# One fixed list orders TensorE, ScalarE and VectorE through the first block of an attention and two-MLP kernel

## The chip, the cores and the metric

The kernel runs on one core of one Trainium2 chip. The metric is the device time of one execution in microseconds (us). The engines are TensorE (PE), VectorE (DVE), ScalarE (ACT), GpSimd (POOL) and SyncE (SP), which issues the transfers.

## The reference, cut to what matters

Three stages follow each other: attention inside chunks of 64 positions, an MLP with a SiLU, and an MLP with a softmax-weighted activation and a normalization. All of it has to come out with float32 accuracy.

```python
# q, k, v: (8, 8, 576, 64); chunks of 64 along the sequence
scores = scale * np.matmul(q_c, k_c.transpose(0, 1, 2, 4, 3))
scores = scores - np.max(scores, axis=-1, keepdims=True)
attn = np.exp(scores)
attn = attn / (np.sum(attn, axis=-1, keepdims=True) + 1e-09)
out = np.matmul(attn, v_c)
# x: (4608, 512); w_in (512, 2048), w_out (2048, 512)
h = x @ w_in
g = h * (1.0 / (1.0 + np.exp(-h)))
x = g @ w_out
# w_in (512, 1024), w_out (1024, 512), g_ln (1024)
h = x @ w_in
e = np.exp(h - np.max(h, axis=-1, keepdims=True))
solu = h * e / (np.sum(e, axis=-1, keepdims=True) + 1e-09)
mu = np.mean(solu, axis=-1, keepdims=True)
var = np.mean((solu - mu) ** 2, axis=-1, keepdims=True)
out = (solu - mu) / np.sqrt(var + 1e-06) * g_ln @ w_out
```

## The kernel before, in words

**Numbers.** Each float32 operand of a matmul is split in two float16 halves, a high one (ACT, L114) and a low one, the rest (POOL at L118 where no gain is applied, else DVE at L119). A product is three matmuls: high by high, high by low, low by high.

**Blocks.** The 4608 rows are taken in nine blocks of 512, each of four tiles of 128. A block b goes through attention, the first layer (16 groups `h_0` to `h_15` of 12 matmuls with w1 and a Silu: `h_group`, and then the halves of its result g: `g_split`), the second layer (w2: `x_part`, four results in two halves of 24 matmuls each), the third (w3: `m_h`, one call a tile, with row maxima, exponentials and the statistics of the normalization on DVE and ACT) and the fourth (w4: `m_out`). The attention of block b + 1 (scores, `a_norm`, P·V with `a_pv`) stands between the parts of block b's second layer; the third and fourth layer of block b - 1 stand between the groups of block b: `m_h` ahead of groups 5, 7, 9 and 11, `m_out` ahead of 13 and 15 and behind 15. Blocks 2 to 8 use another form of the first two layers, with sums of weights that are made during block 1.

**Weights.** The weights come once, as 48 pieces in a line: 0 to 15 are w1, 16 to 31 w2, 32 to 39 w3, 40 to 47 w4. A piece is loaded as 64-bit words and decoded to float32 in four steps: `d1` scales one half on ACT (L133), `d2` shifts and joins the bits with three operations of DVE (L140, L141, L143) and issues the load of a later piece on SP, `d3` makes the halves (ACT at L114, then POOL at L118, or DVE at L119 for w4, which has a gain). `weights(n)` does `d3 d1 d2` n times, each on the oldest piece that waits for it. So the decoding has to stay ahead of its reader: `h_f` needs piece f, the parts of the second layer pieces 16 to 31, `m_h` all of 32 to 39, `m_out` all of 40 to 47.

**What sets the order.** A scheduler puts the instructions of each engine in order by their place in the program and by priorities; `tc.high_priority(offset=-50)` puts what stands inside it later. Only for the start, up to block 0's first group, does a list fix the order: `START` names steps, and each step is issued behind the last instruction of the steps before it, engine by engine (`queue` and `tc.issue_after`). Behind it, `NW0`, `NX`, `NW1` and `NX1` say how many pieces are decoded beside each group of block 0, each step of its second layer, each group of block 1 and each step of that block's second layer. `START` leaves six pieces with d1, five with d2 and four with d3 done; block 0 ends with 37 of d1 and 35 of d3.

**Names in rows.** wst is a loaded piece, wp and wy its decoded forms, w, w2t, w3q, w4h and w4l the halves of weights; qk, qb, qbl and kb belong to the q and k of a tile, vbh and vbl to v, ae and pT to its scores; x is an input of the first layer, g its result; e, u, uT, nmu, c and dv belong to the third layer's activation; y, wq and ws to the sums of weights.

## Time and profile before

| what | value |
|---|---|
| time, median of 3 runs | 1172.4 us (1171.79 to 1173.0) |
| the profiled execution | 1173.64 us, span 1171.9 us |
| mean granted clock of TensorE in it | 0.993 |
| busy in the span: PE, DVE, ACT, POOL | 1123.9, 917.4, 803.3, 250.4 us |

The span is what the profiler's records cover; the execution's own time lies 1.7 us above it. A row of a timeline gives the start in us from the span's start, the duration in us, the engine, the line of the kernel, the operation, what it writes and reads, and shapes. The bracket at its end is the time for which the engine had been idle, and the instruction that ended this, as inferred from semaphores.

### The profile page before, as it was taken

The numbers are of one execution on the slowest core, as the hardware profiler recorded it, in microseconds if no ns is written. First come the engines' busy times: TensorE is split into PE (matmuls) and PEld (weight loads), VectorE is DVE, ScalarE is ACT, GpSimd is POOL, SyncE is SP. The second block draws the span as 40 slices with busy tenths as digits, with TensorE's granted clock in tenths as the row PEclk, the third lists the DMA queues.
The fourth block names the chain that finished last, engine by engine and source line by source line (L and its number), as shares of the span: only waits on it lengthen the run. The fifth ranks groups of instructions, "written<-read, shape, count | busy, mean of one in ns | idle before, by whom it ended". The sixth has DMA issues, their size and how long they took to land.

```text
span 1171.9 us, 23546 instructions
## 1 busy us (share of the span) xinstructions
PE 1123.9 (96%) x9036; PEld 767.0 (65%) x9036; DVE 917.4 (78%) x1639; ACT 803.3 (69%) x1460; POOL 250.4 (21%) x243
## 2 busy tenths in 40 slices
PE   7899898998999999999999999999999999999998
PEld 5344343444657865887678767876787777777853
DVE  6898998587678788889778987898689868886453
ACT  6986678675667777856775687568756875587253
POOL 3655323344101510021003100310021002100001
PEclk8999999999999999999999999999999999999999
DMA  7657488543537654786568557856776667565604
GB/s 280 217 186 209 150 234 270 166 140 113 140 113 222 180 157 132 200 228 179 150 189 235 175 157 192 230 169 160 179 235 173 162 177 223 168 163 145 207 19 117
DMA packets 205169, 209.18 MB, mean 178 GB/s; under 512 B 120192, under 2 KB 130432, under 8 KB 205056
## 3 DMA queue, kind: packets, MB, share of 16 engines
q1 hardware_dynamic: 205056, 207.68, 61.8%
q8 instruction: 70, 1.15, 0.4%
q14 instruction: 43, 0.35, 0.1%
HBM read 156.24 MB, written 24.12 MB: 154 GB/s over the span
## 4 chain that ended last, share of the span: by engine, by line
PE 64%; DVE 13%; ACT 9%; issue 6%; DMA 5%; POOL 2%; ACTq 0%; SPq 0%; POOLq 0%; DVEq 0%
PE o_ps L894 5%; PE o_ps L887 5%; PE o_ps L886 5%; PE pa L655 4%; PE pa L654 4%; PE pa L656 4%; PE pa L547 3%; PE pa L549 3%; PE pa L548 3%; PE pa L781 2%; PE pa L779 2%; PE pa L780 2%; DVE vbl L119 2%; PE pb L549 2%; PE pb L547 2%
## 5 line engine op out<-in xcount | busy, mean ns | idle before, releaser
L114 ACT ACTIVATE q<-hc 128x512 f16<-128x512 f32 x196 | 120.5, 627 | 42.8 <-DVE hc L634 15.6
L119 DVE SCALAR_TENSOR_TENSOR q<-hc,q 128x512 f16<-128x512 f32 x196 | 137.9, 719 | 10.9 <-ACT q L114 8.7
L118 POOL TENSOR_TENSOR qbl<-qk,qbh 64x512 f16<-64x512 f32 x54 | 71.2, 1319 | 264.7 <-ACT qbh L114 220.3
L654 PE MATMUL pa<-q,ring 128*128 128x256 f16 x448 | 122.1, 273 | 0.0
L656 PE MATMUL pa<-q,ring 128*128 128x256 f16 x448 | 122.1, 273 | 0.0
L655 PE MATMUL pa<-q,ring 128*128 128x256 f16 x448 | 122.1, 273 | 0.0
L886 PE MATMUL o_ps<-w4h,uT 128*128 128x512 f16 x288 | 109.1, 379 | 0.3 <-DVE e L837 0.3
L887 PE MATMUL o_ps<-w4l,uT 128*128 128x512 f16 x288 | 109.2, 379 | 0.0
L850 POOL TENSOR_TENSOR c<-c,mhalf 128x2 f32<-128x2 f32 (+1 forms) x22 | 14.1, 639 | 387.3 <-DVE c L849 385.1
L548 PEld LDWEIGHTS <-ring 128*128 128x128 f16 x784 | 77.0, 98 | 16.7 <-issue 6.1
L547 PEld LDWEIGHTS <-ring 128*128 128x128 f16 x784 | 77.0, 98 | 11.3 <-DMA ring<-w1s 0.7
L655 PEld LDWEIGHTS <-ring 128*128 128x128 f16 x784 | 76.7, 98 | 11.1
L654 PEld LDWEIGHTS <-ring 128*128 128x128 f16 x784 | 76.7, 98 | 11.1
L549 PEld LDWEIGHTS <-ring 128*128 128x128 f16 x784 | 77.0, 98 | 9.2
L656 PEld LDWEIGHTS <-ring 128*128 128x128 f16 x784 | 76.7, 98 | 8.8
L894 PE MATMUL o_ps<-w4h,uT 128*128 128x512 f16 x288 | 70.2, 379 | 0.0
L547 PE MATMUL pa<-xb,ring 128*128 128x256 f16 x224 | 61.0, 273 | 3.5 <-DVE hc L605 3.1
L547 PE MATMUL pa<-x,ring 128*128 128x256 f16 x224 | 61.0, 273 | 2.0 <-ACT hc L565 2.0
L549 PE MATMUL pa<-x,ring 128*128 128x256 f16 x224 | 61.2, 273 | 0.0
L549 PE MATMUL pb<-x,ring 128*128 128x256 f16 x224 | 61.1, 273 | 0.0
L548 PE MATMUL pb<-x,ring 128*128 128x256 f16 x224 | 61.1, 273 | 0.0
L654 PE MATMUL pb<-q,ring 128*128 128x256 f16 x224 | 61.1, 273 | 0.0
(282 smaller groups left out, 3483.7 us busy)
## 6 DMA issues: line engine op xcount, KB each, us to landing
ring<-w1s SPq DMA_DIRECT2D x196, 256.0 KB, 3.3
ring<-w2s SPq DMA_DIRECT2D x196, 256.0 KB, 3.7
wst<-w SPq DMA_DIRECT2D x48, 512.0 KB, 4.2
qk<-qkv SPq DMA_DIRECT2D x29, 512.0 KB, 3.9
vs<-qkv SPq DMA_DIRECT2D x36, 256.0 KB, 2.9
out<-o SPq DMA_DIRECT2D x36, 256.0 KB, 2.3
w1s<-ws SPq DMA_DIRECT2D x32, 128.0 KB, 2.0
w2s<-ws SPq DMA_DIRECT2D x16, 256.0 KB, 2.0
```

Source lines behind the costliest of these rows:

```text
L114: ready[0] = A.activation(dst_h, src, AF.Copy, scale=scale).ins
L118: return G.tensor_tensor(out=dst_l, in0=src, in1=dst_h, op=ALU.subtract).ins
L119: return V.scalar_tensor_tensor(out=dst_l, in0=src, scalar=scale, in1=dst_h, op0=ALU.mult, op1=ALU.subtract).ins
L547: T.matmul(ps[:, c], wh, x[:, 0, k], start=first, stop=False, skip_group_check=True)
L548: T.matmul(ps[:, c], wh, x[:, 1, k], start=False, stop=False, skip_group_check=True)
L549: T.matmul(ps[:, c], wl, x[:, 0, k], start=False, stop=k == 1, skip_group_check=True)
L654: T.matmul(ps[:, c], wh, g[:, 0], start=first, stop=False, skip_group_check=True)
L655: T.matmul(ps[:, c], wh, g[:, 1], start=False, stop=False, skip_group_check=True)
L656: T.matmul(ps[:, c], wl, g[:, 0], start=False, stop=q == 1 and f == 3, skip_group_check=True)
L886: T.matmul(ps, uh[:, k], w4h[:, k, :], start=k == 0, stop=False)
L887: T.matmul(ps, uh[:, k], w4l[:, k, :], start=False, stop=False)
L894: T.matmul(ps, ul[:, k], w4h[:, k, :], start=False, stop=k == K2 - 1)
```

## The change

The list now goes on to the end of block 0's second layer. A program of names, `in_order`, runs the steps of `START`, then for each group of block 0 the steps `D h{f} g{f}` and what `BESIDE` gives (D is `d1 d3 d2` of one piece), then the eight strings of `SECOND`, which hold the second layer's parts (X), their halves (Y), block 1's attention (S scores, E exponentials, U sums, N norm, Q the halves of q and k, V those of v, P P·V) and thirteen D. Every instruction of a step on PE, ACT or DVE is held behind the last one of the steps before; POOL and SP are not in the list. `a_scores` and `x_part` are split into steps for it. `START` loses the last five of its decode steps, so it leaves four d1, four d2 and three d3; block 0 ends with 33 of d1 and 32 of d3. `NW1` gives eight pieces to block 1's first four groups (seven went to its first five before). Decoded pieces 16 to 35 lie in other tiles (`ytile`).

```diff
     START = ('s0 m0 s1 m1 e0 s2 s3 e1 n0 m2 m3 d1 t0 e2 p0 n1 e3 a2 n2 t1 x0 t2 n3 p1 d1 d2 x1 d3 l0 t3 l1 p2 x2 d2 '
-             'd1 l2 p3 x3 d3 l3 d2 d1 d3 d2 d1 d3 d2 d1')
+             'd1 l2 p3 x3 d3 l3 d2 d1 d3 d2')
     AT_S = (0, 1, 3, 4)
-    NW0 = [2, 0, 0, 0, 3, 0, 2, 0, 1, 0, 3, 0, 1, 0, 3, 0]
-    NX = [2, 3, 2, 1, 0, 6, 0, 2]
-    NW1 = [2, 1, 2, 1, 1, 1, 1, 1, 1, 1, 1, 1, 1, 1, 1, 0]
-    NX1 = [1, 0, 0, 1, 0, 1, 1, 0]
+    SECOND = ('S0 X0 E0 D U0 N0 D', 'S1 X1 E1 D Q2 D', 'X2 Y0 N1 D D', 'S2 P0 X3 V1 E2 D U2 Q3 D',
+             'S3 P1 X4 Y1 V2 E3 N2 D D', 'X5 N3 D D', 'P2 X6 Y2 V3 D d3', 'P3 X7 Y3')
+    BESIDE = {0: 'L0', 4: 'Q0', 8: 'V0', 11: 'Q1', 15: 'd1'}
+    NW1 = [2, 2, 2, 2, 1, 1, 1, 1, 1, 1, 1, 1, 1, 0, 0, 0]
     MHF = [5, 7, 9, 11]
...
-    def a_scores(t):
+    def a_products(t):
...
+        if whole and part == parts - 1:
+            x_halves(b, d)
+
+    def x_halves(b, d):
+        t = one.tile([P, 2, BLK], F16, tag=f"x2_{d}", name=f"x2_{d}")
+        split(t[:, 0], t[:, 1], xps[d], S_X2 / (S_G * S_W), A, V)
...
     def ytile(i):
-        if i < 28:
-            tag = (None, "q5", "q6", None, "q7")[i % 5] if i < 16 else (None, "x2_1", "x2_2", None, "x2_3")[i % 5]
-            pool, tag = (one, tag) if tag else (two, "o")
-        else:
-            pool, tag = two, "o"
+        tag = (None, "q5", "q6", None, "q7")[i % 5] if i < 16 else f"h{2 + i % 6}" if i < 36 else None
+        pool, tag = (one, tag) if tag else (two, "o")
         return pool.tile([P, 512], I32, tag=tag, name="wy")
...
-    parts = dict(s=f_scores, m=f_max, e=f_exp, a=f_sum, n=f_norm, t=f_turn, p=f_pv, x=f_high, l=f_low)
-    steps = {"d1": d1, "d2": d2, "d3": d3, "w": weights}
+    tile_of = lambda i: TPB + ORDER[i]
+    parts = dict(s=f_scores, m=f_max, e=f_exp, a=f_sum, n=f_norm, t=f_turn, p=f_pv, x=f_high, l=f_low,
+                 h=lambda f: h_group(0, f), g=lambda f: g_split(0, f, GH),
+                 L=lambda i: load_qk(tile_of(i)), Q=lambda i: prep_qk(tile_of(i)), V=lambda i: prep_v(tile_of(i)),
+                 S=lambda i: a_products(tile_of(i)), E=lambda i: a_exp(tile_of(i)), U=lambda i: a_sum(tile_of(i)),
+                 N=lambda i: a_norm(tile_of(i), eng_l=G), P=lambda i: a_pv(tile_of(i), ahead=False),
+                 X=lambda s: x_part(0, s // 2, s % 2, whole=False), Y=lambda d: x_halves(0, d))
+    steps = {"d1": d1, "d2": d2, "d3": d3}
     queue = {}
-    for x in START.split():
-        with ExitStack() as behind_all:
-            for i in queue.values():
-                behind_all.enter_context(tc.issue_after(i))
-            done = steps[x]() if x in steps else parts[x[0]](int(x[1]))
-        for i in done:
-            queue[i.engine] = i
+
+    def in_order(xs):
+        for x in xs.replace("D", "d1 d3 d2").split():
+            traced = nc.cur_bb.bb.instructions
+            last_ = traced[-1]
+            with ExitStack() as behind_all:
+                for i in queue.values():
+                    behind_all.enter_context(tc.issue_after(i))
+                steps[x]() if x in steps else parts[x[0]](int(x[1:]))
+            new = []
+            for i in reversed(traced):
+                if i is last_:
+                    break
+                new.append(i)
+            for i in reversed(new):
+                if i.engine in (mybir.EngineType.PE, mybir.EngineType.Activation, mybir.EngineType.DVE):
+                    queue[i.engine] = i
+
+    in_order(START)
...
-                h_group(b, f)
                 if b == 0:
-                    weights(NW0[f])
-                    if f:
-                        g_split(b, f - 1, GH)
+                    in_order(f"{'D' if f else ''} h{f} g{f} {BESIDE.get(f, '')}")
                 else:
+                    h_group(b, f)
                     y = g_split(b, f, A)
                     with tc.high_priority(offset=-50):
...
+        if b == 0:
+            for xs in SECOND:
+                in_order(xs)
+        elif b < FAST:
```

How it moves instructions is shown at three places. The first is VectorE's order in the middle of block 0's first layer; wp and wy are stages of one piece, g the result of a group. Before:

```order
L140 TENSOR_SCALAR wp_564<-wp_564 128x512
L140 TENSOR_SCALAR wp_607<-wp_607 128x512
L141 SCALAR_TENSOR_TENSOR wp_564<-wst_476,wp_564 128x512
L141 SCALAR_TENSOR_TENSOR wp_607<-wst_550,wp_607 128x512
L143 SCALAR_TENSOR_TENSOR wy_609<-wst_476,wp_564 128x512
L143 SCALAR_TENSOR_TENSOR wy_619<-wst_550,wp_607 128x512
L119 SCALAR_TENSOR_TENSOR g_588<-h_ps_574,g_588 128x512
L119 SCALAR_TENSOR_TENSOR g_641<-h_ps_591,g_641 128x512
```

And after:

```order
L140 TENSOR_SCALAR wp_592<-wp_592 128x512
L141 SCALAR_TENSOR_TENSOR wp_592<-wst_485,wp_592 128x512
L143 SCALAR_TENSOR_TENSOR wy_596<-wst_485,wp_592 128x512
L119 SCALAR_TENSOR_TENSOR g_616<-h_ps_602,g_616 128x512
L140 TENSOR_SCALAR wp_619<-wp_619 128x512
L141 SCALAR_TENSOR_TENSOR wp_619<-wst_512,wp_619 128x512
L143 SCALAR_TENSOR_TENSOR wy_623<-wst_512,wp_619 128x512
L119 SCALAR_TENSOR_TENSOR g_616<-h_ps_629,g_616 128x512
```

Two pieces were decoded side by side and two low halves of g followed them; now a piece is decoded to its end, and one low half of g follows.

The second place is GpSimd's order in the same layer, where the halves of the q and k of block 1's first tile stand among w1's pieces (w1_4 is the fifth piece). Before:

```order
L118 TENSOR_TENSOR w1_3_75<-wy_416,w1_3_75 128x512
L118 TENSOR_TENSOR qbl_114<-qk_858,qbh_113 64x8x64 x2
L118 TENSOR_TENSOR kb_860<-qk_858,kb_860 128x512
L118 TENSOR_TENSOR w1_4_76<-wy_426,w1_4_76 128x512
L118 TENSOR_TENSOR w1_5_77<-wy_462,w1_5_77 128x512
L118 TENSOR_TENSOR w1_6_78<-wy_472,w1_6_78 128x512
```

And after:

```order
L118 TENSOR_TENSOR w1_5_77<-wy_481,w1_5_77 128x512
L118 TENSOR_TENSOR w1_6_78<-wy_508,w1_6_78 128x512
L118 TENSOR_TENSOR qbl_114<-qk_449,qbh_113 64x8x64 x2
L118 TENSOR_TENSOR kb_557<-qk_449,kb_557 128x512
L118 TENSOR_TENSOR w1_7_79<-wy_534,w1_7_79 128x512
L118 TENSOR_TENSOR w1_8_80<-wy_570,w1_8_80 128x512
```

q's and k's halves moved from between pieces 3 and 4 to between pieces 6 and 7.

The third place is VectorE's order in block 1's groups, around the last piece of w4 (wy_2035 before, wy_2166 after) and the activation of a tile of block 0's third layer (c, e, u). Before, where the third tile's row maxima (mp_2067) stand beside it:

```order
L741 TENSOR_REDUCE mp_2067<-h2_ps_2040 128x1
L853 TENSOR_SCALAR e_1919<-e_1919,nmu_1938,c_1943 128x1024
L119 SCALAR_TENSOR_TENSOR g_2030<-g_2028,g_2030 128x512
L741 TENSOR_REDUCE mp_2067<-h2_ps_2041 128x1
L119 SCALAR_TENSOR_TENSOR w4l_109<-wy_1973,gs_110,w4h_108 128x512
L857 TENSOR_TENSOR u_1925<-e_1919,u_1925 128x1024
L743 TENSOR_REDUCE mm__2070<-mp_2067 128x1
L119 SCALAR_TENSOR_TENSOR w4l_109<-wy_2035,gs_110,w4h_108 128x512
L832 TENSOR_SCALAR nm_2073<-mm__2070 128x1
```

And after, where those of the fourth tile (mm__2201) are past:

```order
L746 TENSOR_REDUCE mm__2201<-mp_2198 128x1
L143 SCALAR_TENSOR_TENSOR wy_2166<-wst_2109,wy_2166 128x512
L852 SCALAR_TENSOR_TENSOR c_2074<-dv_2071,c_2074 128x1
L835 TENSOR_SCALAR nm_2204<-mm__2201 128x1
L856 TENSOR_SCALAR e_2050<-e_2050,nmu_2069,c_2074 128x1024
L860 TENSOR_TENSOR u_2056<-e_2050,u_2056 128x1024
L119 SCALAR_TENSOR_TENSOR g_2161<-g_2245,g_2161 128x512
L459 TENSOR_TENSOR y_2254<-wq_2264,y_2254 128x256
L460 TENSOR_TENSOR y_2254<-y_2254,wq_2264 128x256
L119 SCALAR_TENSOR_TENSOR w4l_109<-wy_2166,gs_110,w4h_108 128x512
```

The last low half of w4 stood ahead of the third tile's exponentials; now it stands behind the third tile's u.

## Rows read from the trace of the kernel before

**Rows 1.** The page's first two lines: the span, then busy time of each engine.

```profile
span 1171.9 us, 23546 instructions
...
PE 1123.9 (96%) x9036; PEld 767.0 (65%) x9036; DVE 917.4 (78%) x1639; ACT 803.3 (69%) x1460; POOL 250.4 (21%) x243
```

**Rows 2.** Busy time by stretch: length, PE, PEld, DVE, ACT, POOL; granted clock, DMA.

```profile
24.00:60.00 36.00, 32.10 (x147) 14.27 (x147) 31.28 (x52) 29.66 (x54) 21.87 (x19) 1.00 0.63 216
...
80.00:120.00 40.00, 35.99 (x262) 17.93 (x260) 35.99 (x64) 28.25 (x74) 23.07 (x20) 0.96 0.70 200
120.00:160.00 40.00, 36.78 (x196) 17.59 (x197) 39.01 (x58) 26.63 (x47) 13.89 (x12) 1.00 0.55 171
160.00:200.00 40.00, 33.12 (x161) 15.70 (x161) 36.31 (x82) 34.09 (x62) 15.91 (x19) 1.00 0.91 274
```

**Rows 3.** Timeline of PE, its idle gaps: start, us, instruction, [idle before <-releaser].

```profile
73.38 0.38 PE L716 MATMUL x_ps<-g,w2t 128*128 128x512 f16 x1 [2.91 <-DVE g L119]
...
120.44 0.20 PE L277 MATMUL x_ps<-pT,vbh 128*128 128x64 f16 x1 [2.10 <-ACT vbh L114]
...
128.57 0.38 PE L418 MATMUL h_ps<-x,w 128*128 128x512 f16 x1 [1.26 <-ACT x L114]
...
161.19 0.38 PE L418 MATMUL h_ps<-x,w 128*128 128x512 f16 x1 [1.66 <-ACT g L422]
...
179.33 0.27 PE L447 MATMUL wq<-w,ident 128*128 128x256 f16 x1 [2.86 <-DVE e L837]
...
193.54 0.38 PE L418 MATMUL h_ps<-x,w 128*128 128x512 f16 x1 [2.09 <-DVE y L462]
...
209.09 0.38 PE L886 MATMUL o_ps<-w4h,uT 128*128 128x512 f16 x1 [0.35 <-DVE e L837]
```

**Rows 4.** Timeline of DVE, decoding weight pieces, alone and in pairs.

```profile
23.93 0.69 DVE L140 TENSOR_SCALAR wp<-wp 128x512 int32<-128x512 int32 x1
24.66 0.69 DVE L141 SCALAR_TENSOR_TENSOR wp<-wst,wp 128x512 int32<-128x512 int32 x1
25.39 0.69 DVE L143 SCALAR_TENSOR_TENSOR wy<-wst,wp 128x512 int32<-128x512 int32 x1
...
48.56 1.28 DVE L141 SCALAR_TENSOR_TENSOR wp<-wst,wp 128x512 int32<-128x512 int32 x2
```

**Rows 5.** Timeline of POOL, the halves of a tile's q and k.

```profile
40.52 2.38 POOL L118 TENSOR_TENSOR qb<-qk,qb 64x512 f16<-64x512 f32 x2
42.98 1.16 POOL L118 TENSOR_TENSOR kb<-qk,kb 128x512 f16<-128x512 f32 x1
```

**Rows 6.** Timeline of DVE, a decode operation of a w3 piece.

```profile
122.35 1.66 DVE L141 SCALAR_TENSOR_TENSOR wy<-wst,wy 128x512 int32<-128x512 int32 x1
```

**Rows 7.** Timeline of PE, block 0's first output tile.

```profile
196.46 0.38 PE L886 MATMUL o_ps<-w4h,uT 128*128 128x512 f16 x1
...
199.69 0.38 PE L887 MATMUL o_ps<-w4l,uT 128*128 128x512 f16 x1
199.91 1.89 PE L894 MATMUL o_ps<-w4h,uT 128*128 128x512 f16 x8
```

**Rows 8.** Timeline of DVE, first and last row maxima of block 0's third layer.

```profile
158.02 1.28 DVE L741 TENSOR_REDUCE mp<-h_ps 128x1 f32<-128x512 f32 x2
...
197.02 1.28 DVE L741 TENSOR_REDUCE mp<-h_ps 128x1 f32<-128x512 f32 x2
...
201.29 1.22 DVE L857 TENSOR_TENSOR u<-e,u 128x1024 f16<-128x1024 f32 x1 [1.18 <-ACT u L854]
```

**Rows 9.** Timeline of ACT, the statistics of the third tile of that layer.

```profile
197.20 1.15 ACT L843 ACTIVATE u<-e,nmu 128x1024 f32<-128x1024 f32 x1 [0.66 <-DVE nmu L840]
...
200.20 1.06 ACT L854 ACTIVATE u<-e 128x1024 f16<-128x1024 f32 x1 [0.48 <-DVE e L853]
201.27 1.28 ACT L422 ACT_TABLE_LOAD   x1
202.57 0.60 ACT L422 ACTIVATE g<-h_ps 128x512 f32<-128x512 f32 x1
```

More of the change, by code (lines that the diff above doesn't have):

```diff
@@ L192, in prep_qk @@
     def prep_qk(t, eng_l=G, ahead=True):
-        with ExitStack() as behind_all:
-            if t // TPB == 1:
-                for i in queue.values():
-                    behind_all.enter_context(tc.issue_after(i))
-            qk_halves(t, eng_l, ahead)
-    def qk_halves(t, eng_l, ahead):
         q_, k_ = (y.rearrange("p (s i) -> p s i", s=NS) for y in qk.pop(t))
@@ L210, in prep_v @@
     def prep_v(t):
-        with ExitStack() as behind_all:
-            if t // TPB == 1:
-                for i in queue.values():
-                    behind_all.enter_context(tc.issue_after(i))
-            v_halves(t)
-    def v_halves(t):
         v = vs.pop(t).rearrange("p (s i) -> p s i", s=NS)
@@ L241, in a_scores, with a_exp @@
             V.tensor_scalar(out=m, in0=m, scalar1=-1.0 / 8.0, scalar2=None, op0=ALU.mult)
+        else:
+            V.tensor_tensor(out=e, in0=ps, in1=m.to_broadcast([P, NS, CH]), op=ALU.subtract)
+        et[t] = e, s_, y[:, 1].rearrange("p (h f) -> p h f", h=2), ps, m
+    def a_exp(t):
+        e, s_, ph, ps, m = et[t]
+        if t in EXB:
             for s in range(NS):
@@ L244, in a_scores, with a_sum @@
         else:
-            V.tensor_tensor(out=e, in0=ps, in1=m.to_broadcast([P, NS, CH]), op=ALU.subtract)
             A.activation(e, e, AF.Exp, scale=1.0 / 8.0)
-            V.tensor_reduce(out=s_, in_=e, axis=AX.X, op=ALU.add)
-        et[t] = e, s_, y[:, 1].rearrange("p (h f) -> p h f", h=2)
+    def a_sum(t):
+        if t not in EXB:
+            V.tensor_reduce(out=et[t][1], in_=et[t][0], axis=AX.X, op=ALU.add)
+    def a_scores(t):
+        a_products(t)
+        a_exp(t)
+        a_sum(t)
     def a_norm(t, eng_l=V):
-        e, s_, ph = et.pop(t)
+        e, s_, ph, ps, m = et.pop(t)
         V.tensor_scalar(out=s_, in0=s_, scalar1=1e-9, scalar2=1.0 / S_P, op0=ALU.add, op1=ALU.mult)
@@ L262, in a_norm, with a_pv @@
         pt[t] = pT
-    def a_pv(t):
+    def a_pv(t, ahead=True):
         b, o = divmod(t, TPB)
@@ L279, in a_pv @@
                     T.matmul(o_, vl[:, s], pT[:, 0, 2 * a + c, r], start=False, stop=True)
-        if t % TPB != ORDER[-1]:
+        if ahead and t % TPB != ORDER[-1]:
             prep_v(after(t))
@@ L419, in h_group @@
             T.matmul(ps, wh[:, k], xl[:, k], start=False, stop=False)
-            T.matmul(ps, wl[:, k], xh[:, k], start=False, stop=k == KD - 1)
+            i = T.matmul(ps, wl[:, k], xh[:, k], start=False, stop=k == KD - 1).ins
         g = one.tile([P, BLK], F32, tag=f"h{f % 2}", name="g") if b else ps
-        A.activation(g, ps, AF.Silu, scale=1.0 / (S_X * S_W))
+        j = A.activation(g, ps, AF.Silu, scale=1.0 / (S_X * S_W)).ins
         graw[f] = g
+        return [i, j]
     def g_split(b, f, eng_h=V):
@@ L706, in fused, with x_part @@
     xps = {}
-    def x_part(b, d, part, parts=2):
+    def x_part(b, d, part, parts=2, whole=True):
         if part == 0:
@@ L718, in x_part @@
             T.matmul(ps, wl, gh, start=False, stop=f == K1 - 1)
-        if part == parts - 1:
-            t = one.tile([P, 2, BLK], F16, tag=f"x2_{d}", name=f"x2_{d}")
-            split(t[:, 0], t[:, 1], ps, S_X2 / (S_G * S_W), A, V)
-            for n in range(TPB):
-                x2t[b, n, d] = t[:, 0, n * P:n * P + P], t[:, 1, n * P:n * P + P]
+        if whole and part == parts - 1:
[3 more added lines that the diff above has]
+        split(t[:, 0], t[:, 1], xps[d], S_X2 / (S_G * S_W), A, V)
+        for n in range(TPB):
+            x2t[b, n, d] = t[:, 0, n * P:n * P + P], t[:, 1, n * P:n * P + P]
     ut = {}
@@ L1055, in step @@
             if s == 0:
-                if b < FAST - 1:
-                    load_qk(m)
-                    prep_qk(m)
-                else:
-                    load_qk(after(m))
+                load_qk(after(m))
                 prep_v(m)
-            if b and s == 1:
+            if s == 1:
                 run(m_out(b - 1, MO[TPB - 1]))
@@ L1072, in step @@
                     prep_qk(m + ORDER[i + 1], V if b == 1 else G)
-                a_norm(n, eng_l=V if b else G)
+                a_norm(n)
             if s in AT_P:
@@ L1076, in step @@
                 a_pv(m + ORDER[i])
-            if b == 0:
-                with tc.high_priority(offset=-50):
-                    weights(NX[s])
             if b == FAST and s in W3S:
                 w3_sums(W3S.index(s))
-            if b == 1:
-                weights(NX1[s])
             for n in range(4):
```

10 lines of the change are left out of this document (2 added, 8 removed).

## The prediction, made before the changed kernel ran

> **What bounds the kernel now.** I read the page's totals first. PE is busy for 1123.9 of 1171.9 us [rows 1], so all that an order of instructions can win is in PE's idle time, and the change touches only what runs before about 200 us. The profiled execution took 1173.64 us, 1.24 above the median of the three timed runs (1172.4); I work in differences and take them off the median. About 0.2% (2.3 us) is what a measurement of this kernel tells from no change.
>
> Next came busy time by stretch [rows 2]. PE idles for 3.9 us in 24 to 60, 4.0 in 80 to 120, 3.2 in 120 to 160 and 6.9 in 160 to 200. DVE is idle for 4.7, 4.0, 1.0 and 3.7 us there: it is about as full as PE, and from 120 to 160 fuller. So PE's waits are a second sign of DVE's load, and filling one PE gap moves the wait unless DVE has less to do or idles less.
>
> Third, the waits themselves, in PE's timeline [rows 3]. Block 0's second layer starts at 73.38, after 2.91 us for DVE; the last P·V waits 2.10 us for an ACT half of v; block 1's first group starts at 128.57, after 1.26 us for the last x half; then 1.66, 2.86, 2.09 and 0.35 us, all but the first behind DVE. Those on block 1's side come from one chain: the row maxima of block 0's third layer stand at 158.02 (first tile) and 197.02 (fourth) on DVE [rows 8], in line behind the decoding of w3 and w4. That is the lag to watch: an operation that leaves DVE's line ahead of them brings them forward.
>
> **The change, part by part.**
>
> *Decoding in strict order (block 0).* Before, DVE interleaves two pieces; after, L140, L141 and L143 of one piece follow each other. Where an operation reads what the one before wrote, DVE starts it 0.73 us later (23.93, 24.66, 25.39); two independent ones take 1.28 us together, so the second starts some 0.60 after the first [rows 4]. A piece costs 0.73 + 0.73 + 0.60 = 2.06 us in place of 1.80, so 0.26 more; the list decodes some 27 pieces so: 7.0 us of DVE.
> The Trainium skill ("VectorE: DVE Perf Modes", section "The DRAIN you can't avoid") says that the gap behind each operation is there whether or not operations are chained, so order would cost nothing; by it this term would be 0. The rows differ, 0.73 against 0.60, and I go by them.
>
> *An even beat in the first layer.* Each step is now one piece and one low half of g: 2.06 + 0.60 = 2.66 us of DVE, where PE needs 2.59 for 12 matmuls (12 at 0.216 between starts, as in [rows 7]: 3.23 us for fifteen starts). Against that, POOL makes the pieces' low halves in its own order. The halves of q and k of a tile are 2.38 + 1.16 = 3.54 us there [rows 5]; they stand ahead of w1's piece 7 now, and of piece 14 the second time. With one piece of slack in hand I get PE stalls of some 2.2 us at h_7 and 2.5 at h_14 (bounds: 0 if POOL has idled enough, 3.5 if no slack). The first layer then ends near 70.0, and its second layer starts at some 70.8, 2.6 us earlier than now, since the 2.91 us wait [rows 3] goes.
>
> *The second layer and block 1's attention.* The 2.10 us wait at the last P·V goes: v's halves stand two parts earlier. In place of it come waits for pieces behind POOL's q and k: x part 2 behind the third tile's (up to 3.5 us [rows 5]), the fourth scores behind the fourth tile's (some 3 us), and parts 1 and 5 for a piece each (some 2.3 us). PE's own work between the two starts of now, 73.38 and 128.57, is some 47.1 of 55.2 us: eight halves of 24 matmuls at 0.216, 41.4, and an estimated 5.7 for scores and P·V, the rest being waits and lost clock. So 70.8 + 47.1 + 10 of waits puts block 1 at 127.9, where it starts at 128.57 now (the four waits are bounded by 0 and 11). The granted clock (0.96 in 80 to 120 now [rows 2]) is taken as whole. So PE gains 0.7 here (bounds: a loss of 1, a gain of 4).
>
> *Fewer pieces ahead of block 1.* The order has 181 DVE operations up to block 1's last x half in place of 186, and 220 in place of 227 up to the first row maximum (five decode operations and two low halves of w4 fewer). Five at 0.60 are 3.0 us and the two halves 1.4 (by a low half's 0.70; up to 2.2 where POOL runs beside them). Of the DVE idle of some 8.7 us in the two stretches of [rows 2], what is recovered pays the 7.0 us of strict order. So the first maximum comes 4.4 to 7 us earlier than 158.02. From there to the fourth it has 76 operations in place of 73, with four more of decoding: 2.4 us by 0.60 each, up to 5 if POOL stretches them as it did L141 of a w3 piece, to 1.66 [rows 6]. Some of the 3.7 us of idle in 160 to 200 is filled instead. I take the lead at the fourth maximum as 6 us (197.02 becomes 191.0), with bounds 4 and 7.5. On PE the 1.66 us wait goes and those of 2.86 and 2.09 shrink by about 3, so PE could start the first output tile at some 191 (196.46 now).
>
> *The new wait: w4's last piece.* The first output tile reads piece 7 of w4 in its last matmuls of L889 and L890, 3.2 us after its start, with eight of L897 behind it [rows 7]. Before, all eight pieces are ready ahead of the fourth maximum. After, the last piece's high half stands on ACT behind the third tile's square, a k half, a table load, a Silu, the high half of u, one of g, a copy and another Silu; its low half stands on DVE behind the third tile's u. Counted from the maximum's start, ACT's square begins at +0.18 and takes 1.34 with its accumulator; then k's half 0.6 (by the Silu's 0.60), one half as wide 0.33, the table load 1.28, the Silu 0.5 to the next start, the high half of u 1.06 [rows 9]: +5.3. DVE's u takes 1.2 [rows 8], a half of g 0.6, two operations half as wide 0.6 and the low half 0.7: +8.4. With the maximum at 191.0 that is 199.4. The tile then ends nine starts of 0.216 later, at 201.35; now it ends at 199.91 + 8 x 0.216 = 201.64 [rows 7]. PE stands for 5 us behind this one half, and h_13 and all later groups stand behind it. So of the 5 us that PE could have had, 0.3 are left.
>
> *After it.* The wait of 0.35 at the second output tile [rows 3] goes, since its tile's statistics now come earlier. From DVE's 362nd operation the two orders have the same counts; nothing later changes. The number of fetches is the same 48; each is issued behind its piece's L143 as before, one per beat, and I cost the other tiles for decoded pieces at nothing: their old readers are done by the order.
>
> *Sum:* 201.35 - 201.64 - 0.35 = -0.6 us: 1171.8. With a lead of 4 it is 1173.8, with 7.5 it is 1170.3.
>
> **The rivals.**
> *A, the gaps really close.* If POOL's q and k halves cost PE half of what I count (15 us in six places), block 1 starts some 4 us earlier, DVE with it, and the last w4 piece moves 1:1: 1168. For it: POOL idles in most of 24 to 60 (21.9 busy of 36 [rows 2]). Against it: DVE has 7.0 us more to do by its spacing. It decides from a lead of 7.7 us.
> *A', spacing costs nothing,* as the skill's page has it: DVE gains 7 us, PE some 5, and the time is 1167. The 0.73 against 0.60 in [rows 4] speaks against it.
> *B, the w4 piece is later still (slower).* Each us by which the fourth maximum leads less than 6 costs one. Fifteen decode operations instead of eleven between the first and the fourth maximum, if each takes 1.2 to 1.66 beside POOL [rows 6], bring the lead to 2: 201.64 + 4 - 0.35 - 0.3 = 3.4 later, 1175.8; with no lead it is 1177.8. It decides from a lead of about 3.1.
> *C, the order changes nothing that counts:* what leaves the front of DVE's line comes back behind it in kind, 1172.4.
>
> **How the numbers follow.** My forecast has 0.37 (0.32 within 0.2%, 0.02 faster, 0.03 slower), its own range 1170 to 1174. A has 0.31, A' 0.04, B 0.23, C 0.05. Faster is 0.02 + 0.31 + 0.04 = 0.37, no change 0.32 + 0.05 = 0.37, slower 0.03 + 0.23 = 0.26. The range takes in A and B to their middle and a little beyond: 1166.5 to 1177, with 1 in 10 out on each side.
>
> **What would show it.** In the profile after: DVE starts at 0.73, 0.73, 0.60 in the h groups; PE waits at h_7 and h_14 and behind POOL's q and k in the second layer; a start of the second layer near 70.8, of block 1 near 127.9; maxima near 152 and 191; and in the first output tile, at its last L889 or L890, a wait of some 5 us for w4h or w4l. If that wait is under 2 us and the tile ends before 199, A holds; if it ends after 204, B. I am wrong in mechanism if the stalls lie elsewhere, above all if block 1's start has moved by more than 3 us.

## The result: 0.9% slower, and the profile after

The changed kernel takes 1183.5 us (median of 5 runs, 1182.4 to 1183.9) against 1172.55 for the kernel before beside it (1171.8 to 1173.9): a ratio of 1.0091, 95% interval 1.0076 to 1.0106. Forecast were 1171.8 and a range of 1166.5 to 1177. The span of the profiled execution grows by 10.1 us, to 1182.0. The page after; only 2.7 us of the growth are PE's busy time, the rest is idle (compare [rows 1]):

```profile
span 1182.0 us, 23538 instructions
...
PE 1126.6 (95%) x9036; PEld 764.4 (65%) x9036; DVE 923.9 (78%) x1639; ACT 804.6 (68%) x1460; POOL 251.0 (21%) x243
```

PE's timeline after, the gaps that answer to [rows 3], then the first output tile of [rows 7]:

```profile
46.35 0.39 PE L419 MATMUL h_ps<-x,w 128*128 128x512 f16 x1 [1.07 <-POOL w L118]
...
67.63 0.61 PE L419 MATMUL h_ps<-x,w 128*128 128x512 f16 x1 [1.83 <-POOL w L118]
...
94.05 0.39 PE L718 MATMUL x_ps<-g,w2t 128*128 128x512 f16 x1 [1.93 <-POOL w2t L118]
...
106.79 0.19 PE L219 MATMUL s_ps<-kb,qb 128*128 128x64 f16 x1 [2.79 <-POOL kb L118]
...
133.09 0.38 PE L417 MATMUL h_ps<-x,w 128*128 128x512 f16 x1
...
153.27 0.59 PE L738 MATMUL h_ps<-w3q,x 128*128 128x512 f16 x2 [2.05 <-ACT w3q L114]
154.56 0.81 PE L738 MATMUL h_ps<-w3q,x 128*128 128x512 f16 x3 [0.69 <-POOL w3q L118]
...
199.88 0.38 PE L889 MATMUL o_ps<-w4h,uT 128*128 128x512 f16 x1
...
210.37 0.58 PE L889 MATMUL o_ps<-w4h,uT 128*128 128x512 f16 x1 [7.31 <-ACT w4h L114]
211.46 0.59 PE L890 MATMUL o_ps<-w4l,uT 128*128 128x512 f16 x1 [0.50 <-DVE w4l L119]
211.84 2.97 PE L897 MATMUL o_ps<-w4h,uT 128*128 128x512 f16 x8
214.65 0.38 PE L417 MATMUL h_ps<-x,w 128*128 128x512 f16 x1
```

Block 1 starts at 133.09, 4.5 us later than before; the third layer's first call waits 2.74 us for w3, a wait that the kernel before does not have; the first output tile starts 3.4 us later (199.88 against 196.46), and 7.31 us pass inside it for the last piece of w4. The group behind it starts at 214.65, 13.0 us after the 201.64 of before. So 4.5 us are lost by block 1's start, 1.1 regained up to the output tile (66.8 us from 133.09 to 199.88, before 67.9 from 128.57 to 196.46) and 9.6 lost in it; 2.9 come back by the end.

Busy time by stretch after, first two stretches of [rows 2], then four short ones:

```profile
24.00:60.00 36.00, 34.70 (x147) 14.81 (x147) 30.88 (x48) 28.89 (x50) 16.88 (x15) 0.92 0.58 187
80.00:120.00 40.00, 31.40 (x234) 14.68 (x231) 34.30 (x58) 26.78 (x71) 21.98 (x20) 0.96 0.57 165
...
22.40:29.50 7.10, 5.93 (x15) 2.07 (x15) 5.48 (x9) 3.72 (x7) 2.31 (x2) 0.53 0.69 218
64.00:71.50 7.50, 5.24 (x18) 1.74 (x17) 6.67 (x11) 5.61 (x12) 5.70 (x5) 0.77 0.74 234
107.60:113.00 5.40, 5.40 (x40) 2.46 (x37) 4.75 (x10) 4.59 (x21) 0.26 (x1) 0.68 0.92 294
210.30:214.70 4.40, 3.83 (x11) 1.31 (x11) 3.32 (x6) 2.23 (x6) 2.60 (x3) 0.58 1.16 217
```

DVE has fewer operations in 24 to 60 (48, before 52) and in 80 to 120 (58, before 64), and yet idles longer: 5.1 and 5.7 us, before 4.7 and 4.0. The four short stretches are PE's slow ones. DVE's timeline after, one step of the first layer and then the maxima and the last piece of w4:

```profile
51.49 0.69 DVE L140 TENSOR_SCALAR wp<-wp 128x512 int32<-128x512 int32 x1
52.21 0.69 DVE L141 SCALAR_TENSOR_TENSOR wp<-wst,wp 128x512 int32<-128x512 int32 x1
53.01 0.69 DVE L143 SCALAR_TENSOR_TENSOR wy<-wst,wp 128x512 int32<-128x512 int32 x1
53.62 0.68 DVE L119 SCALAR_TENSOR_TENSOR g<-h_ps,g 128x512 f16<-128x512 f32 x1
...
162.11 1.28 DVE L744 TENSOR_REDUCE mp<-h_ps 128x1 f32<-128x512 f32 x2
...
200.07 0.68 DVE L744 TENSOR_REDUCE mp<-h_ps 128x1 f32<-128x512 f32 x1
...
208.25 1.23 DVE L860 TENSOR_TENSOR u<-e,u 128x1024 f16<-128x1024 f32 x1 [1.42 <-ACT u L857]
...
210.66 0.75 DVE L119 SCALAR_TENSOR_TENSOR w4l<-wy,gs,w4h 128x512 f16<-128x512 f32 x1
```

ACT's timeline after, what stands ahead of the high half of that piece:

```profile
201.00 1.15 ACT L846 ACTIVATE u<-e,nmu 128x1024 f32<-128x1024 f32 x1
...
204.95 0.42 ACT L114 ACTIVATE ws<-y 128x256 f16<-128x256 f32 x1 [2.19 <-DMA w1s<-ws]
205.38 1.28 ACT L421 ACT_TABLE_LOAD   x1
...
207.17 1.05 ACT L857 ACTIVATE u<-e 128x1024 f16<-128x1024 f32 x1
...
209.59 0.73 ACT L114 ACTIVATE w4h<-wy,gs 128x512 f16<-128x512 f32 x1
```

The first maximum is 4.1 us later than in [rows 8] and the fourth 3.05, where leads of 4.4 to 7 and of 6 us were forecast.

### The profile page after: what moved, and what is told of

It is laid out like the page before. It is cut to its first block, busy times and chain, and to the rows that moved or that the text cites. A ratio compares the mean times of both kernels' runs of the same rounds, so it can differ in the third digit from the quotient of the medians.

```text
span 1182.0 us, 23538 instructions
## 1 busy us (share of the span) xinstructions
PE 1126.6 (95%) x9036; PEld 764.4 (65%) x9036; DVE 923.9 (78%) x1639; ACT 804.6 (68%) x1460; POOL 251.0 (21%) x243
## 4 chain that ended last, share of the span: by engine, by line
PE 64%; DVE 13%; ACT 7%; issue 4%; DMA 2%; POOL 1%; SPq 1%; ACTq 0%; POOLq 0%; DVEq 0%
PE o_ps L897 5%; PE o_ps L890 5%; PE o_ps L889 5%; PE pa L655 4%; PE pa L656 4%; PE pa L654 4%; PE pa L547 3%; PE pa L549 3%; PE pa L548 3%; PE pa L784 2%; PE pa L782 2%; PE pa L783 2%; DVE vbl L119 2%; PE pb L547 1%; PE pb L548 1%
## 5 line engine op out<-in xcount | busy, mean ns | idle before, releaser
L654 PEld LDWEIGHTS <-ring 128*128 128x128 f16 x784 | 76.7, 98 | 10.9
L547 PE MATMUL pa<-x,ring 128*128 128x256 f16 x224 | 61.0, 272 | 3.6 <-ACT hc L565 2.8
L547 PE MATMUL pb<-x,ring 128*128 128x256 f16 x224 | 61.1, 273 | 0.2 <-DMA ring<-w1s 0.2
L549 PE MATMUL pb<-x,ring 128*128 128x256 f16 x224 | 61.1, 273 | 0.0
L548 PE MATMUL pb<-x,ring 128*128 128x256 f16 x224 | 61.1, 273 | 0.0
```

The source lines that it names most:

```text
L547: T.matmul(ps[:, c], wh, x[:, 0, k], start=first, stop=False, skip_group_check=True)
L548: T.matmul(ps[:, c], wh, x[:, 1, k], start=False, stop=False, skip_group_check=True)
L549: T.matmul(ps[:, c], wl, x[:, 0, k], start=False, stop=k == 1, skip_group_check=True)
L654: T.matmul(ps[:, c], wh, g[:, 0], start=first, stop=False, skip_group_check=True)
```

## The experiments

Each percentage is against the kernel before, run beside it; a percent is 11.7 us. The change stands at +0.91% (+0.76 to +1.06).

**w4_ahead.** The decoding beside the first seven groups of block 1 gets a priority that puts w4's pieces earlier:

```diff
-                    with tc.high_priority(offset=-50):
+                    with tc.high_priority(offset=-50 if f < 7 else 100):
```

> The changed kernel with one edit: from block 1's seventh group on, the decoding of weights gets a higher priority in place of a lower one, so the last low half of w4 stands ahead of the fourth row maximum on VectorE instead of behind the third tile's u. Nothing else moves by more than a few places. Theory A: the 7.3 + 0.5 us for which TensorE stands in the first output tile, and the half clock in its last nine matmuls (1.7 us), are a cost of their own, from the place of w4's last piece alone; then the wait there is under 1 us and the time is 8 us less than the changed kernel's, 1175.5 (1174 to 1177). Rival B: w4's place is only where the lateness of VectorE and ScalarE shows; then the wait comes back at the third layer or the second output tile, and the time stays above 1180.

Measured: 1179.8 us, +0.57% (0.36 to 0.78). The wait in the output tile is gone, and some 4 of 10.7 us with it; the time lies between A's and B's. PE's timeline of this kernel shows where other waits stand now:

```profile
176.15 1.02 PE L738 MATMUL h_ps<-w3q,x 128*128 128x512 f16 x4 [2.79 <-DVE y L462]
...
199.03 0.38 PE L417 MATMUL h_ps<-x,w 128*128 128x512 f16 x1 [1.69 <-DVE y L462]
```

The output tile is 9.6 us shorter than in the change (207.12 - 201.94 = 5.18 between the first starts, there 14.77) and the gain less than half of that: the rest is waited for elsewhere, mostly behind DVE. So the last piece of w4 is a part of the loss and not the whole.

**out_later.** The first output tile is called one group later: `MOF = [14, 15]` in place of `[13, 15]`.

> The changed kernel with the first output tile one group later on TensorE (ahead of block 1's fifteenth group, not its fourteenth), with w4's last piece where it is. Theory A (the wait is for w4's last piece, whose time does not hang on TensorE): one group of 12 matmuls and the sums beside it, 2.6 to 3.1 us, are done inside the wait, which shrinks from 7.3 to some 4.5 us; the time is 2 to 3 us less, 1180.5 to 1181.5. Rival B (VectorE and ScalarE bound the whole of block 1's groups): the time stays within 1 us of 1183.5.

Measured: 1181.1 us, +0.61% (0.40 to 0.81). One group more (12 matmuls, up to 201.6) runs ahead of the tile, as A has it, and PE then waits 3.92 and 1.67 us, where the change waits 7.31 and 0.50: the time is in A's range. The waits now stand ahead of the tile and behind ACT. PE's timeline:

```profile
206.35 0.37 PE L447 MATMUL wq<-w,ident 128*128 128x256 f16 x1 [3.92 <-ACT g L421]
...
208.39 0.59 PE L889 MATMUL o_ps<-w4h,uT 128*128 128x512 f16 x1 [1.67 <-ACT y L454]
```

**more_ahead.** Three more pieces in the second layer (`SECOND` ends with `'P2 X6 Y2 V3 D D', 'P3 X7 Y3 D D d1'`), and `NW1 = [2, 2, 2, 2, 2, 2, 2, 1, 1, 0, 0, 0, 0, 0, 0, 0]`, so that the later pieces follow sooner too.

> The changed kernel with three more pieces decoded inside the list, at the end of the second layer, and the rest of them pulled to block 1's first nine groups, so block 0 ends with about as many pieces as before the change (37 scaled, 34 with both halves) and the last low half of w4 stands well ahead of the fourth maximum. Theory A: the wait in the first output tile goes as well, VectorE pays some 5 us more inside the second layer, of which TensorE sees 1 to 3: 1175 to 1178. Rival B (VectorE's lateness shows wherever it can): above 1180.

Measured: 1180.9 us, +0.64% (0.46 to 0.83). The output tile runs without a wait (202.39 to 207.57), but the w3 wait does not shrink: it grows from 2.74 to 5.25 us. PE's timeline has it in three pieces:

```profile
152.58 0.38 PE L738 MATMUL h_ps<-w3q,x 128*128 128x512 f16 x1 [2.78 <-ACT w3q L114]
154.50 1.01 PE L738 MATMUL h_ps<-w3q,x 128*128 128x512 f16 x2 [1.55 <-POOL w3q L118]
156.44 0.58 PE L738 MATMUL h_ps<-w3q,x 128*128 128x512 f16 x1 [0.92 <-ACT w3q L114]
```

**long_start.** The five decode steps are put back at the end of `START`.

> The changed kernel with the longer first list of before, which decodes two pieces more ahead of the first group. Theory A: the half clock from 22.4 to 29.5 us, which makes the first layer's first group and a half 3.3 us longer, comes from how the first list ends; with the old end TensorE's clock is full when the groups begin, as it was before, and the time is 3 to 4 us less than the changed kernel's, some 1180. Rival B: where the clock falls in the first 30 us does not hang on the end of the list; then the time is within 1 us of 1183.5, and the slow stretch is again behind 22 us or wherever TensorE has idled.

Measured: 1184.4 us, +0.93% (0.76 to 1.10), no change. B holds: PE's clock is again near its lower level in 22 to 30 (0.57), so the end of the first list does not set it there. Nor is the start of the chain of pieces what costs: the fourth scores now wait 5.61 and 2.77 us for kb.

**q3_early** (on top of w4_ahead). The halves of the fourth tile's q and k stand one part earlier:

```diff
-    'X2 Y0 N1 D D', 'S2 P0 X3 V1 E2 D U2 Q3 D',
+    'X2 Y0 N1 D Q3 D', 'S2 P0 X3 V1 E2 D U2 D',
```

> The kernel with w4's pieces ahead with one edit: the halves of the fourth tile's q and k stand one string earlier in the list, behind the norm of the second tile and one piece, so GpSimd makes them some 7 us sooner. Theory A: TensorE's 0.84 + 2.79 us ahead of the fourth scores are a matter of that place alone, and the half clock behind them (1.5 to 1.8 us) goes with them: 4 to 5 us less, some 1175. Rival B: GpSimd's line is what is short there; w2's pieces then come 3.5 us later in their turn, TensorE waits for them at the second layer's parts 2 to 4 by as much, and the time stays within 1.5 us of 1179.8.

Measured: 1181.5 us, +0.63% (0.47 to 0.78), against +0.57 without. The wait at the fourth scores goes and comes back at two pieces of w2. PE's timeline:

```profile
102.75 0.39 PE L718 MATMUL x_ps<-g,w2t 128*128 128x512 f16 x1 [2.01 <-POOL w2t L118]
...
114.36 0.39 PE L716 MATMUL x_ps<-g,w2t 128*128 128x512 f16 x1 [2.70 <-ACT w2t L114]
```

**fill** (on top of w4_ahead). Ahead of the fourth scores PE runs 15 matmuls on finished w1 halves, whose result the scores overwrite:

```diff
+        if t == TPB + ORDER[3]:
+            for i in range(15):
+                T.matmul(ps.rearrange("p s i -> p (s i)"), w1t[i][:, 0, 0], w1t[i][:, 1].rearrange("p k f -> p (k f)"), start=True, stop=True)
```

> The kernel with w4's pieces ahead, with 15 matmuls of 512 columns put into TensorE's wait ahead of the fourth scores; they write the scores' own tile, which is then written anew, so they add no result and take 3.2 of the 3.6 us for which TensorE stands there. Theory A: the clock falls to half behind that wait because TensorE stood still; with the filling it stays whole through the fourth and fifth part of the second layer, which then take 1.5 to 1.8 us less, and the time is 1 to 2 us less than 1179.8. Rival B: the half clock there comes with something else; it stays, and the time is the same or up to 1 us more.

Measured: 1180.8 us, +0.55% (0.40 to 0.70): no gain that can be told, though the 1 to 2 us of A are only 0.09 to 0.17%, less than the intervals are wide. Windows of w4_ahead, then the same two of this kernel:

```profile
100.00:106.00 6.00, 2.37 (x45) 1.64 (x44) 5.02 (x9) 2.84 (x5) 5.69 (x5) 0.98 0.40 115
106.00:114.00 8.00, 7.67 (x38) 3.18 (x35) 6.91 (x14) 7.28 (x25) 1.98 (x2) 0.80 0.69 224
```

```profile
100.00:106.00 6.00, 5.43 (x49) 2.86 (x48) 5.12 (x8) 3.29 (x6) 5.39 (x5) 1.00 0.33 119
106.00:114.00 8.00, 6.56 (x53) 2.98 (x49) 7.12 (x14) 7.14 (x25) 2.15 (x3) 1.00 0.73 231
```

PE's clock stays at its upper level behind the gap, 0.80 becomes 1.00, and PE then waits 1.24 and 0.69 us for w2 at 113.19 and 114.49: a faster PE reaches the next wait sooner. From the second layer's start to block 1's it takes 59.35 us (72.31 to 131.66), in w4_ahead 59.74 (71.86 to 131.60).

**pairs** and **pairs_q3_early** (on top of w4_ahead). The list decodes two pieces side by side, as the kernel before does, at every second step (`d1 d1 d3 d2p d3`; d2p is L140 twice, L141 twice, L143 twice); the second kernel has q3_early's edit too.

> The kernel with w4's pieces ahead (1179.8 us) with one edit: inside the list two pieces are decoded at a time, their six VectorE operations taking turns (L140 twice, L141 twice, L143 twice), where they stood one piece after the other. As many operations, and as many pieces, in block 0. Theory A: the strict order costs VectorE some 0.13 us for each dependent pair of operations, 5 to 7 us up to block 1, and that is why it comes to the third layer late; with pairs VectorE's starts lie 0.60 apart, the first row maximum moves from some 161 to 157 or before, and the time is 3 to 6 us less, 1174 to 1177. Rival B: VectorE's spacing is not what holds it up, but waits on ScalarE and GpSimd that the list ties it to; the spacing goes to 0.60, its idle time grows by the same, and the time stays within 1.5 us of 1179.8.

> The pairs and the earlier halves of q and k together. Theory A (each wait is its own place): the gains add, 1170 to 1174, level with the kernel before the change or better. Rival B (what is taken from one wait comes back at the next, since VectorE has the same work and ScalarE and GpSimd stay tied to it): above 1176.

Measured: +1.60% (1.44 to 1.77) and +1.50% (1.33 to 1.67), far slower. Pieces come in bursts and the groups wait for them (2.08 us for w at 45.80, 2.15 at 75.66; 5.27 for kb at 117.33), so these two do not price the spacing. They show one thing beside it: with the decoding at 0.6 us from start to start, DVE stands idle for ACT's halves of g in its place (1.22 us at 49.58, 0.42 at 50.70, and the same at 56.19 and 57.31), as B of pairs has it.

**free_both, free_dve, free_act, free_after.** Behind `START`, the list holds PE alone (free_both), PE and ACT (free_dve), or PE and DVE (free_act); the engines that are left out go by the scheduler's order. These three have w4_ahead's edit; free_after is free_both without it, so the change with its list kept on PE only.

```diff
-                if i.engine in (mybir.EngineType.PE, mybir.EngineType.Activation, mybir.EngineType.DVE):
+                if i.engine in held:
...
+    free = (mybir.EngineType.PE,)
```

> The kernel with w4's pieces ahead (1179.8 us), with the list behind the first block's start binding TensorE alone: the same steps in the same program order, the same pieces beside the same groups, but on ScalarE and VectorE the scheduler may let steps overlap. On VectorE one piece's L141 and the next one's L140 then stand between two dependent operations. Theory A: it is the fixed order on ScalarE and VectorE that makes VectorE late (dependent operations 0.73 apart, and each engine waiting for the other at a step's end): VectorE's starts go to 0.60, the idle time of TensorE between the second layer's start and block 1's falls from 10 us to 6 or less, the first row maximum comes 4 to 8 us sooner, and the time is 5 to 9 us less, 1171 to 1175. Rival B: it is what the program asks for that costs (w3's pieces beside block 1's groups, GpSimd's q and k halves, the smaller start), whatever the order: the time stays above 1177.

> The same with the list binding TensorE and ScalarE, VectorE free. Theory A with VectorE's dependent spacing as the cause: nearly all of the gain of freeing both, 1172 to 1176. Theory A2, ScalarE's waits for steps of the list as the cause: little, above 1177.

> The same with the list binding TensorE and VectorE, ScalarE free. Theory A with VectorE's spacing as the cause: little, above 1177. Theory A2, ScalarE's waits as the cause: nearly all of the gain, 1172 to 1176.

> The changed kernel itself (w4's pieces not put ahead, 1183.5 us) with the list binding TensorE alone. By its order the last low half of w4 again stands behind the fourth maximum. Theory A, in which VectorE's lateness makes the wait in the first output tile: with VectorE sooner by 4 to 8 us that wait shrinks from 7.8 to under 4, and the time is 6 to 10 us less, 1174 to 1178. If the wait hangs on w4's place alone, it stays above 6, and the time is 3.7 us above that of the same kernel with w4 ahead.

Measured: free_both 1173.9 us, +0.02% (-0.08 to +0.11), level with the kernel before; free_dve +0.65% (0.50 to 0.80); free_act +0.38% (0.24 to 0.52); free_after 1176.9 us, +0.25% (0.14 to 0.36). So the list's hold on ACT and DVE and the place of w4's pieces make up the loss between them, 0.91% with both and 0.02% with neither; what free_both keeps of the change (the counts, the shorter `START`, the other tiles) costs nothing on the whole. DVE's timeline of free_both, in the first layer:

```profile
51.43 0.69 DVE L141 SCALAR_TENSOR_TENSOR wp<-wst,wp 128x512 int32<-128x512 int32 x1
52.02 0.69 DVE L140 TENSOR_SCALAR wp<-wp 128x512 int32<-128x512 int32 x1
52.63 0.68 DVE L143 SCALAR_TENSOR_TENSOR wy<-wst,wp 128x512 int32<-128x512 int32 x1
```

Operations of two pieces alternate and start 0.6 us apart. Block 1 starts at 125.92 in free_both and at 124.82 in free_after, where it starts at 131.60 with the list on three engines and w4 ahead, and at 133.09 in the change. In free_after the last low half of w4 still stands behind the fourth maximum on DVE, but both are early enough: its first output tile runs through, 198.80 to 203.98.

free_dve does not bring the 0.6 us back in the first layer: DVE's starts there are 47.32, 48.05, 48.85 and 49.45, the strict order still. free_act keeps the strict order too (47.80, 48.53, 49.33, 49.93), and yet block 1 starts at 127.92 in it and the first maximum stands at 158.42, against 131.60 and 160.63 with w4 ahead.

The freed kernel is not faster than before, though it starts block 1 2.6 us sooner. PE's timeline of free_both:

```profile
146.18 0.59 PE L738 MATMUL h_ps<-w3q,x 128*128 128x512 f16 x2 [0.89 <-ACT w3q L114]
147.94 0.59 PE L738 MATMUL h_ps<-w3q,x 128*128 128x512 f16 x2 [1.17 <-POOL w3q L118]
...
182.72 0.27 PE L447 MATMUL wq<-w,ident 128*128 128x256 f16 x1 [4.29 <-DVE e L840]
```

The first output tile starts at 199.23, 2.8 us later than before: between the two points 5.4 us are lost again, 2.06 of them for w3. This execution took 1176.4 us, 2.5 above the median of its kernel, so a part of the 5.4 can be its own.

**free_first, free_second** (both with w4 ahead). The list holds PE only in the first layer, or only behind it.

> The same with TensorE alone bound through the first layer and all three engines behind it. Theory A (second layer): 1178 to 1180. Rival B (first layer): 1174 to 1176. If both kernels stand halfway, each layer has its share.

> The kernel with w4's pieces ahead (1179.8 us), all three engines bound through block 0's first layer and TensorE alone through its second layer and block 1's attention. Theory A, the cost sits in the second layer, where exponentials, halves and decoding take turns in steps: nearly all of the 5.9 us, 1174 to 1176. Rival B, it sits in the first layer's beat (dependent operations of VectorE, one piece a group): 1178 to 1180.

Measured: +0.32% (0.21 to 0.43) and +0.29% (0.19 to 0.40), each about half of the way from +0.57 to +0.02. Both layers have their share.

**free_more, free_long, free_long_more.** free_both with more_ahead's three pieces back in the second layer, with long_start's five steps, and with both, to take the w3 wait away.

> The kernel whose list binds TensorE alone (with w4's pieces ahead, 1173.9 us), with three more pieces decoded at the end of block 0's second layer and the counts beside block 1's groups of before. Theory A: TensorE's 2.1 us for w3 ahead of the first tile of the third layer, and the lateness behind it, come from w3's pieces beside block 1's groups; with more of them done before, the wait is under 1 us, the first row maximum stays near 158 or sooner, and the time is 1 to 3 us less, 1171 to 1173, level with or just under the kernel before. Rival B: VectorE has the same work up to the third layer wherever it stands; the three pieces put off block 1's start by what is saved behind it, and the time stays within 1 us of 1173.9.

> The same kernel with the longer first list of before (two pieces further ahead at the first group) and everything else as it is. Theory A: with one or two w3 pieces more done in block 0, the w3 wait shrinks: 1172 to 1173.5. Rival B: the longer start puts off the first group by as much: within 1 us of 1173.9 or above.

> Both together, so that block 0 ends with two pieces more than in the kernel before. Theory A: no wait for w3 is left and the time is 1170.5 to 1172.5, less than before. Rival B: block 1 starts later by 2 to 3 us and the time stays within 1 us of 1173.9.

Measured: +0.20% (0.11 to 0.30), +0.36% (0.22 to 0.51), +0.22% (0.11 to 0.34): all slower than free_both. (free_more and free_long_more have `NW1` as in the kernel before.) In free_more the w3 wait is as long as it was (0.89 and 1.17 us). In free_long and free_long_more it is gone, but block 1 starts at 132.38 and 132.89, 6.5 and 7.0 us later than in free_both, as B has it. Over the five kernels whose list holds PE alone, block 1 starts anywhere from 124.8 to 132.9 and the first output tile from 197.9 to 200.2 (before: 128.57 and 196.46). So a start of block 1 that is earlier or later by some us hardly moves what stands behind it.

**before_fewer.** The kernel before with fewer pieces ahead of block 1: `NX = [2, 3, 2, 1, 0, 5, 0, 0]` and the change's `NW1`.

> The kernel before the change with its counts alone altered: three pieces fewer beside block 0's second layer and the counts of the changed kernel beside block 1's groups; no list, the other steps of block 1 as they were. Theory A, moved pieces cost as such: 2 to 5 us more, 1175.5 to 1178.5. Rival B: without a list the scheduler puts the decoding where VectorE is free whatever the counts say (its order hardly moves: the fourth maximum stands at place 297 and the last low half of w4 at 285, as before), and the time stays within 1 us of the kernel before.

Measured: 1177.2 us, +0.32% (0.20 to 0.44). The first maximum does not move (158.18, before 158.02), since the scheduler puts DVE's operations in the same order up to there. The fourth comes at 200.26, 3.2 us later: 1.5 of them are there at 162.69, after a gap of 3.00 us (1.66 before), and the rest is a gap of 4.39 us at 183.68 behind DVE's e, after a small change of ACT's order (halves of block 2's q stand at 174.16, before at 187.56). The time lies in A's range, but the path is not A's, so it settles neither theory; it shows how much two such places are worth.

## Why the prediction was wrong, step by step

The prediction named a sign of being wrong in mechanism: stalls elsewhere, above all a start of block 1 that has moved by more than 3 us. It moved by 4.5, and the first output tile ended after 204, where it put rival B.

**Spacing of dependent operations: right.** 0.72, 0.80 and 0.61 us between the starts, 2.13 a piece (forecast 2.06); where nothing holds DVE to one piece at a time, 0.6 each. The trace does not agree with the rule of the Trainium skill ("VectorE: DVE Perf Modes", "The DRAIN you can't avoid"), which has the same gap with and without chaining: 0.72 and 0.80 us against 0.6.

**The stalls of the first layer: right in place, smaller in size.** h_7 1.07 and h_14 1.83 us, forecast 2.2 and 2.5. That the first is so small is in part luck: PE came late to it by its low clock in 22.4 to 29.5, and in out_later, whose clock was whole there, it is 1.88.

**The failed step: "what is recovered [of DVE's idle time] pays the 7.0 us of strict order".** Nothing was recovered. These windows run from 24 to the start of the second layer and to that of block 1, before, then after, then to block 1's in free_after:

```profile
24.00:73.38 49.38, 42.58 (x215) 19.34 (x215) 43.19 (x71) 40.21 (x73) 26.50 (x23) 1.00 0.63 211
24.00:128.57 104.57, 91.42 (x576) 43.83 (x575) 93.71 (x154) 80.23 (x166) 57.77 (x50) 0.98 0.64 202
```

```profile
24.00:74.56 50.56, 47.00 (x215) 19.98 (x215) 43.55 (x67) 40.73 (x71) 25.56 (x23) 0.91 0.61 197
24.00:133.09 109.09, 96.57 (x576) 43.58 (x576) 95.63 (x149) 80.48 (x163) 54.77 (x48) 0.94 0.61 188
```

```profile
24.00:124.82 100.82, 94.11 (x576) 43.53 (x576) 93.40 (x151) 78.40 (x162) 55.45 (x48) 0.95 0.64 200
```

Up to block 1, DVE idles for 10.9 us before and for 13.5 after, with five operations fewer; with PE alone held it is 7.4 (free_after) and 8.8 (free_both). In the prediction's terms, 4.4 us less work and 7.0 of strict order put the first maximum 2.6 us later if no idle time pays; it came 4.1 later, where 4.4 to 7 earlier were forecast. (The 0.4 us by which DVE idles longer in 24 to 60 proves nothing alone: in w4_ahead, with the same list, it idles for 4.1 us there, less than before.)

I had summed each engine's work as if the list only chose an order. It also ties an engine's next step to its own program order, so a wait on one engine stands in front of work that it could have done. Freeing ACT and DVE takes 0.66% off without and 0.55% off with w4 ahead (0.91 to 0.25, 0.57 to 0.02): 7.7 and 6.4 us, the largest part of the 10.7. That much is shown. How it comes about is in part argued, since freeing both gives DVE's 0.6 us spacing back as well, and that term alone was put at 7.0; no run changes it alone. The waits for ACT in pairs and the earlier block 1 of free_act, where the spacing is still strict, speak for the tie. But free_act's gain in time, 0.19%, is not clear of the intervals, and what the spacing is worth stays open.

**The second layer: the waits as forecast, its start and PE's own work not.** From its start to block 1's PE idles for 9.0 us (10 forecast) and is busy for 49.6 (47.1 forecast, at a whole clock), and the start is 74.56 and not 70.8. So 3.8 us late, 2.5 more of work and 1.0 less of waits make the 5.2 by which block 1 misses 127.9. Waits moved from part to part, with q3_early and fill too.

**"The granted clock is taken as whole": wrong, and the smaller part of the cause.** Up to the second layer's start PE's idle time falls from 6.8 to 3.6 us, as the even beat was to bring, but the same 215 matmuls keep it busy for 47.0 us and not 42.6, at 0.91 of the full clock: the clock takes back more than the waits gave. The experiments tell how much of that reaches block 1. In w4_ahead and out_later the list is the same up to there and the clock is 0.97 up to the second layer; that layer starts at 71.86 and 72.92, and block 1 1.5 and 0.6 us sooner than in the change. In w4_ahead the clock is 0.97 from 24 to block 1's start, about the 0.98 of before, and block 1 is still 3.0 us late. So about a third of the 4.5 us goes with the clock. Behind waits it was 0.77 (64 to 71.5), 0.68 (107.6 to 113) and 0.58 (210.3 to 214.7). At the first place it stayed whole in w4_ahead (1.00 in 64 to 71.5), behind the same wait of 1.83 us, and the second layer starts 5.5 us after that wait and not 6.9. At the second place filling the gap made it whole, and 0.4 us less pass from the second layer's start to block 1's (fill). In the output tile it adds 1.25 us (3.19 from 211.46 to 214.65, for nine starts of 0.216).

**The wait that I did not see.** The third layer's first call waits 2.74 us for w3. The term "fewer pieces ahead of block 1" counted DVE's operations and not that the pieces left over are read so soon. Here it costs little by itself: waits of 1.66, 2.86 and 2.09 us behind it [rows 3] shrink to one of 2.45 in turn, so the stretch is no longer than before.

**The lead at the fourth maximum: the sign was wrong.** 6 us early were forecast, 3.05 late were measured; block 1's start alone is 4.5 later.

**w4's last piece: mechanism right, size not.** It was ready 11.3 us after the fourth maximum's start (211.41 against 200.07), not 8.4: the square began at +0.93 instead of +0.18, and ACT stood 2.19 us for a transfer ahead of ws that the working left out; the two make 2.9. So the tile's end, forecast at 201.35, follows: 9.05 for the maximum, 2.9 for the chain and 1.25 for the clock give 214.55; it is 214.65. It is rival B, whose bound of no lead was passed by 3 us. Putting the pieces earlier is worth 0.34% with the list on three engines. With it on PE alone it is worth 0.23%, though no wait stands in the tile there (free_after), so that part is not this wait's price.

**Still open.** Why free_both needs 73.3 us from block 1's start to the first output tile (before 67.9): the w3 wait is 2.06 of it, and where the pieces put back took that wait away, block 1 started later by more. What binds the stretch up to the first output tile, whenever block 1 starts, no run shows. And why 2.9 us return after the first output tile.

## What to carry to other kernels

A list that fixes the order on several engines is more than a choice of order: each engine then stands behind its own next step, and one late half can hold up work that has no part in it. Hold the engine whose order matters (here PE) and leave the others free: that alone took some 7 of 10.7 us back. Work that is moved out of a full stretch is only late work: name its next reader, and when that reader now runs.
